# Converting float64 weights 1024 columns at a time, with the sign restored by two leaky ScalarE passes

## The chip, the cores and the metric

The kernel runs on one core of a Trainium2 chip. The metric is the device time of one execution in microseconds; the time before is the median of three runs. The profile is of one further execution on the same kind of chip, taken by the hardware profiler. TensorE (PE) multiplies matrices, VectorE (DVE) and ScalarE (ACT) work elementwise, GpSimd (POOL) does some sums, and SyncE (SP) issues every transfer in one queue.

## The reference

```python
scores = (q_c @ k_c.T) / sqrt(64)          # blocks of 64 tokens, 4 x 8 heads, 576 tokens
attn = exp(scores - max(scores)); attn /= sum(attn) + 1e-9
x = (attn @ v_c)                           # as (2304 tokens) x 512
h = x @ moe_w_in                           # 512 -> 2048
x = (s * relu(h)**2 + b) @ moe_w_out       # 2048 -> 512
h = x @ moe2_w_in
out = (relu(h) + log1p(exp(-abs(h)))) @ moe2_w_out
```

The four weight matrices arrive as float64, because scaling by a float64 square root made them so. The kernel reads each float64 as two 32-bit words and makes a float32 of it.

## The kernel before

The work is written as a list of operations. Each has a key (the time at which it is wanted), a cost on each engine that may run it, the operations that it follows and the places in memory that it takes. A planner (`Work.order`) goes through that list with these costs and writes the order of every engine's instructions: at each step it takes the operation that can start first, and among those that can start at the same time the one with the lowest key. The order is fixed when the program is built; on the chip each engine runs its own list in order and waits on semaphores.

The stages, by the core's time: attention over 18 tiles of 128 tokens with the first products of the first layer mixed in (to about 110 us); the first layer's product with `w_in` by seven-product sums of blocks (`quad`, to about 268 us); its product with `w_out` in six blocks (`block`, to 470 us); the second layer's `w_in` (to about 620 us) and its `w_out` (`second_by_blocks`). Each float32 operand is split into a high and a low part (`split`: a ScalarE copy, L505, and a VectorE difference, L514) and multiplied three times.

`convert` makes float32 out of 512 columns of float64 on 128 partitions: a load of 512 KB into a word buffer `f` (two of them, 1024 words each), then, with `hi` and `lo` the two words,

- o1 (L400, VectorE): `(hi >> 20) & 0x7FF`, the exponent, into the scratch buffer `am` (one, 1024 words: half for the exponent, half for the mantissa);
- o2 (L417, ScalarE): Relu that moves the exponent to float32's place and bias;
- o3 (L430, VectorE): `hi & 0xFFFFF | 0x100000`, the mantissa;
- o4 (L444, VectorE): mantissa plus `lo` times 2^-32;
- o5 (L458, VectorE): the sign of `hi` put into the exponent word;
- o6 (L472, VectorE): mantissa times exponent, into the destination.

`weights1` calls it twice for each of the eight slices of an input matrix, into the buffer `wf` (one), then makes four sums on GpSimd (L492) and splits the results. `weights2` calls it twice for each of eight slices of an output matrix. For the first layer (`ph` 0) the result goes to one of three buffers and is stored to `spill`; for the second (`ph` 1) there is one destination at `AT_S2`, four GpSimd sums are made beside it and three stores take it to `forms2`. The same memory is later used by the second layer's `quad` for `s2`, which therefore waits for all these stores (`free_from["s2"]`).

So there are 64 conversions: 16 each for the two matrices of both layers. `turn` keeps those of one stream in order; a load's key lies 12 us ahead of its conversion (`LEAD_F`). The activation table for the exponential is loaded at the start, the one for the second layer's softplus once, at its first use.

Of the kernel before, what the change touches and what calls it, by code (L numbers as in the profile page):

```python
# [8 lines left out]
F32 = mybir.dt.float32  # L9
F32R = mybir.dt.float32r  # L10
U32 = mybir.dt.uint32
# [7 lines left out]
P = 128  # L19
B, H, S, D = 4, 8, 576, 64  # L20
NT = B * S
DM = H * D
# [193 lines left out]
def block_attention_two_layers(  # L216
# [113 lines left out]
    PLACES = {"A": 2, "S": 3, "at": 3, "wf": 1, "f": 2, "am": 1, "s2": 2, "dd": 2, "go": NGO}  # L330
# [6 lines left out]
    base = {"wf": (AT_WF, 2048), "f": (AT_F, 1024), "am": (AT_AM, 1024), "s2": (AT_S2, N)}  # L337
# [41 lines left out]
    def convert(ph, c, part, key, dst, uses=(), w=(), gone=()):  # L379

        chain = "f", part
        f, am = Place("f"), Place("am")
        src = lambda: (w1, w2)[ph][c, part].bitcast(U32)
        ld = load(
            key - LEAD_F,
            lambda: at(f).bitcast(U32),
            src,
            2 * P * DM * 4,
            deps=gone,
            uses=[*uses, f],  # L390
            after=turn.get(chain, ()),
        )
        turn[chain] = [ld]
        words = lambda: at(f).bitcast(U32).rearrange("p (a b) -> p a b", b=2)
        a = lambda: at(am)[:, :DM].bitcast(U32)
        m = lambda: at(am)[:, DM:].bitcast(U32)
        o1 = add(
            {"DVE": dve(DM, True)},
            key,
            lambda e: nc.vector.tensor_scalar(  # L400
                out=a(),
                in0=words()[:, :, 1],
                scalar1=20,
                scalar2=0x7FF,
                op0=ALU.logical_shift_right,
                op1=ALU.bitwise_and,
            ),
            [ld],
            [f, am],
# [3 lines left out]

        o2 = add(
            {"ACT": act(DM)},
            key,
            lambda e: nc.scalar.activation(  # L417
                out=a().bitcast(I32),
                in_=a().bitcast(I32),
                func=AF.Relu,  # L420
                scale=float(1 << 23),
                bias=-float(896 << 23),
            ),
            [o1],
            [am],
        )
        o3 = add(
            {"DVE": dve(DM, True)},
# [10 lines left out]
            [f, am],  # L439
        )  # L440
        o4 = add(
            {"DVE": dve(DM)},
            key,
            lambda e: nc.vector.scalar_tensor_tensor(  # L444
                out=m().bitcast(F32),
# [7 lines left out]
            [f, am],  # L453
        )
        o5 = add(
            {"DVE": dve(DM)},
            key,
            lambda e: nc.vector.scalar_tensor_tensor(  # L458
                out=a(),
                in0=words()[:, :, 1],  # L460
                scalar=0x80000000,
                in1=a(),
# [1010 lines left out]
```

## Time and profile before

| | |
|---|---|
| Time, median of 3 runs | 830.0 us (829.66 to 830.26) |
| Profiled execution, first to last instruction | 834.3 us |
| PE busy | 795.1 us (95%) |
| DVE busy | 654.0 us (78%) |
| ACT busy | 506.4 us (61%) |
| POOL busy | 148.6 us (18%) |
| Moved by DMA | 180.26 MB, 216 GB/s |

The profile gives no time of its execution other than the span from the first to the last instruction, which is 0.5% above the median of the timed runs. Busy shares are means over stages with different limits, so they don't tell what bounds a stage. Transfers and the reading of the queue are not part of busy time.

### The profile page before, as it was taken

To read this page: it belongs to the slowest core of one execution; us is meant where nothing else is said; L and a number is where in the kernel's file an instruction comes from. 1 tells how busy PE (TensorE), PEld (TensorE's weight loads), DVE (VectorE), ACT (ScalarE), POOL (GpSimd) and SP (SyncE) were. 2 spreads that over 40 slices of the span, in tenths; PEclk is the share of its full clock that TensorE was granted. 3 is DMA by queue.
4 is the path that set the end of the run, shared out by engine and by line. 5 is a ranking of instruction groups with operands and counts; after the bars stand their busy time and mean duration, and the time that the engine had idled before them with its cause. 6 is when DMAs were issued, how large, how long until landed. Compare 5 with 4: busy or idle time off the path is not lost.

```text
span 834.3 us, 14524 instructions
## 1 busy us (share of the span) xinstructions
PE 795.1 (95%) x5117; PEld 775.0 (93%) x5117; DVE 654.0 (78%) x1174; ACT 506.4 (61%) x1076; POOL 148.6 (18%) x162
## 2 busy tenths in 40 slices
PE   4688889999999999999999989999999999999998
PEld 3577789999998999999999989999999999999997
DVE  5799888888967869888888776778784767777865
ACT  3655555666656877767767655555555655555543
POOL 4254240111111003222213540111110000000000
PEclk9899999999999999999999999999999999999999
DMA  8665347868757835767662027657667996688851
GB/s 235 195 190 170 106 144 241 262 240 269 257 218 275 324 107 161 244 225 255 224 197 88 11 95 262 232 197 251 246 233 253 354 372 226 203 262 297 277 187 57
DMA packets 80632, 180.26 MB, mean 216 GB/s; under 512 B 9008, under 2 KB 53040, under 8 KB 79664
## 3 DMA queue, kind: packets, MB, share of 16 engines
q1 hardware_dynamic: 80560, 179.34, 63.9%
q8 instruction: 40, 0.66, 0.3%
q14 instruction: 32, 0.26, 0.1%
HBM read 111.15 MB, written 68.16 MB: 215 GB/s over the span
## 4 chain that ended last, share of the span: by engine, by line
PE 83%; DVE 8%; DMA 3%; ACT 3%; issue 1%; POOL 1%; SPq 0%; ACTq 0%; DVEq 0%
PE at L916 17%; PE S L916 10%; PE S L1093 9%; PE at L1093 9%; PE S L1244 8%; PE at L1244 8%; PE A L916 7%; PE A L1093 6%; PE A L1244 5%; DVE operands L514 2%; DVE mem L492 2%; PE at L852 2%; PE at L733 1%; DMA mem<-in_w_dram 1%; DMA last<-in_k_dram 1%
## 5 line engine op out<-in xcount | busy, mean ns | idle before, releaser
L492 POOL TENSOR_TENSOR mem<-mem 128x256 f32<-128x256 f32 x120 | 109.6, 923 | 414.1 <-DVE mem L472 309.2
L514 DVE TENSOR_TENSOR operands<-mem,operands 128x384 fp32r<-128x384 f32 (+4 forms) x186 | 130.9, 720 | 45.0 <-ACT operands L505 43.1
L505 ACT CAST operands<-mem 128x384 fp32r<-128x384 f32 (+4 forms) x186 | 112.3, 620 | 58.8 <-PE at L1244 36.1
L514 DVE TENSOR_TENSOR operands<-last,operands 128x384 fp32r<-128x384 f32 (+2 forms) x184 | 110.5, 616 | 42.4 <-ACT operands L505 39.9
L505 ACT CAST operands<-last 128x384 fp32r<-128x384 f32 (+2 forms) x184 | 94.3, 528 | 73.2 <-PE A L1093 46.5
L916 PE MATMUL at<-operands 128*128 128x384 f32 x624 | 122.4, 340 | 4.1 <-ACT mem L350 2.0
L916 PEld LDWEIGHTS at<-operands 128*128 128x128 f32 x624 | 110.4, 190 | 6.7 <-ACT mem L350 2.7
L1093 PE MATMUL S<-operands 128*128 128x384 f32 x432 | 90.7, 335 | 0.4 <-DVE operands L514 0.4
L1093 PE MATMUL at<-operands 128*128 128x384 f32 x432 | 90.3, 334 | 0.0
L1244 PE MATMUL S<-operands 128*128 128x384 f32 x384 | 87.4, 334 | 0.1
L1244 PE MATMUL at<-operands 128*128 128x384 f32 x384 | 87.1, 334 | 0.0
L916 PE MATMUL S<-operands 128*128 128x384 f32 x420 | 83.5, 337 | 0.9 <-DVE S L492 0.8
L1093 PEld LDWEIGHTS S<-operands 128*128 128x128 f32 x432 | 76.2, 188 | 0.9 <-DVE operands L514 0.6
L1093 PEld LDWEIGHTS at<-operands 128*128 128x128 f32 x432 | 76.2, 188 | 0.0
L948 ACT ACTIVATE mem<-S 128x384 f32<-128x384 f32 x104 | 50.6, 492 | 41.1 <-PE S L916 34.4
L916 PEld LDWEIGHTS S<-operands 128*128 128x128 f32 x420 | 73.5, 188 | 1.5 <-DVE S L492 1.3
L1244 PEld LDWEIGHTS S<-operands 128*128 128x128 f32 x384 | 68.3, 188 | 0.4 <-DVE operands L514 0.4
L1244 PEld LDWEIGHTS at<-operands 128*128 128x128 f32 x384 | 68.3, 188 | 0.0
L916 PE MATMUL at<-last,operands 128*128 128x384 f32 x336 | 67.2, 337 | 0.6 <-ACT S L938 0.2
L492 DVE TENSOR_TENSOR mem<-mem 128x384 f32<-128x384 f32 (+1 forms) x108 | 60.7, 589 | 9.1 <-ACT mem L948 7.8
L1093 PE MATMUL A<-operands 128*128 128x384 f32 x288 | 65.4, 334 | 0.0
L916 PE MATMUL A<-operands 128*128 128x384 f32 x300 | 60.5, 341 | 3.3 <-ACT S L938 1.5
(79 smaller groups left out, 1217.0 us busy)
## 6 DMA issues: line engine op xcount, KB each, us to landing
mem<-in_w_dram SPq DMA_DIRECT2D x64, 512.0 KB, 4.4
summed<-mem SPq DMA_DIRECT2D x168, 192.0 KB, 2.3
mem<-summed SPq DMA_DIRECT2D x30, 768.0 KB, 4.8
hid<-mem SPq DMA_DIRECT2D x96, 192.0 KB, 2.9
last<-hid SPq DMA_DIRECT2D x24, 768.0 KB, 5.3
last<-summed SPq DMA_DIRECT2D x12, 768.0 KB, 4.9
mem<-forms SPq DMA_DIRECT2D x7, 1024.0 KB, 7.1
last<-in_q_dram SPq DMA_DIRECT2D x18, 256.0 KB, 4.2
```

What stands on the lines that cost most here:

```text
L492: lambda e: on(e).tensor_tensor(out=out(), in0=x(), in1=y(), op=op or ALU.subtract),
L505: lambda e: nc.scalar.copy(out=hi().bitcast(F32R), in_=x()),
L514: lambda e: nc.vector.tensor_tensor(out=lo().bitcast(F32R), in0=x(), in1=hi(), op=ALU.subtract),
L733: nc.tensor.matmul(out_[c * D : (c + 1) * D, pr], of("q")[:, pr * P + c * D : pr * P + (c + 1) * D], kb[:, :, pr, c, :], start=True, stop= ...
L852: nc.tensor.matmul(at(px)[y, x], of("v")[y, x], of("aT")[y, x], start=True, stop=True)
L916: nc.tensor.matmul(acc(dst)().rearrange("p (u c) -> p u c", u=GROUP), l[a], r[c], start=start and kk == 0 and x == 0, stop=kk == 1 and x == 2,
L948: lambda e: nc.scalar.activation(out=at(go), in_=acc(place)(), func=AF.Softplus if ph else AF.Relu),
L1093: nc.tensor.matmul(at(accs[d])[:, :N], l[a], r[c], start=m == 0 and z == 0, stop=m == NM - 1 and z == 2,)
L1244: nc.tensor.matmul(at(accs[d])[:, :N], l[a], r[c], start=i == 0 and y == 0, stop=i == NF - 1 and y == 2,)
```

## The change

Two chunks of 512 columns are converted together. The word buffer `f` becomes one of 2048 words that takes two loads; the scratch `am` holds the exponents of all 1024 columns, and the mantissa is made in the destination instead. For three of the four matrices the shift is arithmetic and keeps the sign (so exponent and sign are one number), and two ScalarE passes with a leaky function (slope 1 on one side, 2^-40 on the other, which rounding drops) turn that number into the float32 word with its sign; the first of them writes over the words, so it follows o4. For the second layer's input matrix the steps stay as they were, 1024 columns wide. The first layer's `weights2` gets a word buffer of its own at `AT_XO` and two destinations in place of three; the second layer's keeps its one destination, which is now written from o3 on.

```diff
-    PLACES = {"A": 2, "S": 3, "at": 3, "wf": 1, "f": 2, "am": 1, "s2": 2, "dd": 2, "go": NGO}
+    PLACES = {"A": 2, "S": 3, "at": 3, "wf": 1, "f": 1, "am": 1, "s2": 2, "dd": 2, "go": NGO}
...
-    base = {"wf": (AT_WF, 2048), "f": (AT_F, 1024), "am": (AT_AM, 1024), "s2": (AT_S2, N)}
+    base = {"wf": (AT_WF, 2048), "f": (AT_F, 2048), "am": (AT_AM, 1024), "s2": (AT_S2, N)}
...
-    def convert(ph, c, part, key, dst, uses=(), w=(), gone=()):
+    def convert(ph, i, part, key, dst, uses=(), w=(), gone=(), words_at=None):
...
+        am, uses = Place("am"), list(uses)
+        if words_at is None:
+            place = Place("f")
+            f, held, fw = lambda: at(place), [place], []
+        else:
+            f, held, fw = lambda: mem(words_at, 2048), [], [(words_at, 2048)]
+        ld = []
+        for y in range(2):
+            c = 2 * i + (y if part else 1 - y)
+            ld.append(
+                load(
+                    key - LEAD_F,
+                    lambda y=y: f()[:, y * 1024 : (y + 1) * 1024].bitcast(U32),
+                    lambda c=c: (w1, w2)[ph][c, part].bitcast(U32),
+                    2 * P * DM * 4,
+                    deps=gone,
+                    uses=[*uses, *held],
+                    after=ld or turn.get(chain, ()),
+                    w=[(z + y * 1024, 1024) for z, _ in fw],
+                )
+            )
+        turn[chain] = ld[1:]
+        words = lambda: f().bitcast(U32).rearrange("p (a b) -> p a b", b=2)
+        a, m, n = lambda: at(am).bitcast(U32), lambda: dst().bitcast(U32), 2 * DM
+        signed = not (ph and part == 0)
...
-                scalar2=0x7FF,
-                op0=ALU.logical_shift_right,
+                scalar2=-1 if signed else 0x7FF,
+                op0=ALU.arith_shift_right,
...
             [o1],
-            [f, am],
+            [*held, *uses],
+            r=fw,
+            w=w,
...
+        if signed:
+
+            y = lambda: f()[:, :n]
+            o2 = add(
+                {"ACT": act(n)},
+                key,
+                lambda e: nc.scalar.activation(
+                    out=y(), in_=a().bitcast(I32), func=AF.Prelu, scale=-1.0, bias=-896.0, alpha=2.0**-40
+                ),
+                [o1, o4],
+                [am, *held],
+                w=fw,
+            )
+            o5 = add(
+                {"ACT": act(n)},
+                key,
+                lambda e: nc.scalar.activation(
+                    out=a().bitcast(I32),
+                    in_=y(),
+                    func=AF.Prelu,
+                    scale=-(2.0**63),
+                    bias=-float(1792 << 23),
+                    alpha=2.0**-40,
+                ),
+                [o2],
+                [am, *held],
+                r=fw,
+            )
...
-        c1 = convert(ph, 2 * i + 1, 0, key, lambda: at(wf)[:, :DM], [wf])
-        c0 = convert(ph, 2 * i, 0, key + 0.1, lambda: at(wf)[:, DM : 2 * DM], [wf])
+        c0 = c1 = convert(ph, i, 0, key, lambda: at(wf)[:, : 2 * DM], [wf])
...
-        x = ((AT_XO, 3) if ph == 0 else (AT_S2, 1))
-        a = x[0] + i % x[1] * 2 * DM
+        a = AT_S2 if ph else AT_XO + 2048 + i % 2 * 2 * DM
...
+        c = [convert(ph, i, 1, key, lambda: mem(a, 2 * DM), (), span, gone, None if ph else AT_XO)]
```

## Rows read from the trace of the kernel before

**Rows 1.** The page: busy time by engine, and the chain that ended last.

```profile
PE 795.1 (95%) x5117; PEld 775.0 (93%) x5117; DVE 654.0 (78%) x1174; ACT 506.4 (61%) x1076; POOL 148.6 (18%) x162
...
PE 83%; DVE 8%; DMA 3%; ACT 3%; issue 1%; POOL 1%; SPq 0%; ACTq 0%; DVEq 0%
```

**Rows 2.** Busy time by stretches: from:to, length, PE, PEld, DVE, ACT, POOL busy, clock, DMA, GB/s.

```profile
0.00:40.00 40.00, 22.32 (x229) 17.93 (x229) 25.54 (x50) 19.94 (x96) 13.97 (x23) 0.94 0.78 221
40.00:98.00 58.00, 50.13 (x754) 43.24 (x752) 54.74 (x107) 33.36 (x68) 25.53 (x27) 0.95 0.49 152
112.00:140.00 28.00, 26.43 (x147) 24.82 (x146) 24.05 (x42) 16.47 (x34) 4.72 (x5) 1.00 0.63 211
140.00:240.00 100.00, 99.34 (x569) 98.69 (x568) 88.68 (x149) 62.34 (x124) 14.78 (x17) 1.00 0.77 256
290.00:470.00 180.00, 180.00 (x1041) 180.00 (x1040) 150.18 (x270) 123.68 (x251) 46.01 (x46) 1.00 0.55 177
```

**Rows 3.** Groups by line, the conversion: count | busy us, mean ns | idle before.

```profile
L458 DVE SCALAR_TENSOR_TENSOR mem<-mem 128x512 uint32<-128x512 uint32 x64 | 46.0, 719 | 1.8 <-ACT mem L417 1.7
L444 DVE SCALAR_TENSOR_TENSOR mem<-mem 128x512 f32<-128x512 uint32 x64 | 45.8, 716 | 0.7
L472 DVE SCALAR_TENSOR_TENSOR mem<-mem 128x512 f32<-128x512 f32 x64 | 44.1, 688 | 1.0
...
L417 ACT ACTIVATE mem<-mem 128x512 int32<-128x512 int32 x64 | 40.3, 630 | 10.1 <-DVE mem L400 9.8
...
L400 DVE TENSOR_SCALAR mem<-mem 128x512 uint32<-128x512 uint32 x64 | 35.3, 552 | 5.5 <-DMA mem<-in_w_dram 4.5
L430 DVE TENSOR_SCALAR mem<-mem 128x512 uint32<-128x512 uint32 x64 | 33.3, 521 | 0.0
```

**Rows 4.** Groups by line and shape: instructions of 1024 columns.

```profile
L514 DVE TENSOR_TENSOR operands<-mem,operands 128x1024 fp32r<-128x1024 f32 x22 | 27.6, 1256 | 4.2 <-ACT operands L505 4.2
...
L505 ACT CAST operands<-mem 128x1024 fp32r<-128x1024 f32 x22 | 23.1, 1050 | 0.4 <-POOL mem L492 0.4
```

**Rows 5.** Line 400, the shift: least, median and greatest duration in ns.

```profile
L400 DVE TENSOR_SCALAR mem<-mem x64: 411/426/1032, 7.9 to 609.5; 128x512 uint32<-128x512 uint32 x64
```

**Rows 6.** Groups by line, VectorE, from 33 to 98 us.

```profile
L458 DVE SCALAR_TENSOR_TENSOR mem<-mem 128x512 uint32<-128x512 uint32 x2 | 2.2, 1121 | 0.0
...
L444 DVE SCALAR_TENSOR_TENSOR mem<-mem 128x512 f32<-128x512 uint32 x2 | 2.0, 988 | 0.0
L472 DVE SCALAR_TENSOR_TENSOR mem<-mem 128x512 f32<-128x512 f32 x2 | 1.5, 739 | 0.0
L400 DVE TENSOR_SCALAR mem<-mem 128x512 uint32<-128x512 uint32 x2 | 1.4, 725 | 0.5 <-DMA mem<-in_w_dram 0.5
...
L430 DVE TENSOR_SCALAR mem<-mem 128x512 uint32<-128x512 uint32 x2 | 0.8, 396 | 0.0
```

**Rows 7.** Line 430, from 140 to 240 us.

```profile
L430 DVE TENSOR_SCALAR mem<-mem x22: 414/422/967, 142.8 to 237.3; 128x512 uint32<-128x512 uint32 x22
```

**Rows 8.** Timeline, 331 to 471 us: start, duration, engine, line, operation.

```profile
331.89 2.89 SPq L367 DMA_DIRECT2D forms<-mem  x3
...
399.11 0.69 DVE L472 SCALAR_TENSOR_TENSOR mem<-mem 128x512 f32<-128x512 f32 x1
...
404.03 2.43 POOL L492 TENSOR_TENSOR mem<-mem 128x256 f32<-128x256 f32 x3 [3.18 <-DVE mem L472]
...
407.27 1.92 SPq L367 DMA_DIRECT2D forms<-mem  x3
...
414.51 0.68 DVE L472 SCALAR_TENSOR_TENSOR mem<-mem 128x512 f32<-128x512 f32 x1
...
439.91 1.47 SPq L367 DMA_DIRECT2D forms<-mem  x3
...
470.69 3.28 PE L916 MATMUL at<-operands 128*128 128x384 f32 x18
```

**Rows 9.** Timeline, ScalarE at 475 us: a table load.

```profile
475.08 1.28 ACT L948 ACT_TABLE_LOAD   x1 [0.20 <-issue]
```

More of the change, by code (lines that the diff above doesn't have):

```diff
@@ L377, in block_attention_two_layers @@
     turn = {}
-    def convert(ph, c, part, key, dst, uses=(), w=(), gone=()):
+    def convert(ph, i, part, key, dst, uses=(), w=(), gone=(), words_at=None):
         chain = "f", part
[L382 to L396, printed above, removed]
+        am, uses = Place("am"), list(uses)
[23 more added lines that the diff above has]
+        signed = not (ph and part == 0)
@@ L412, in convert @@
         turn["am", part] = [o1]
[L414 to L426, printed above, removed]
         o3 = add(
-            {"DVE": dve(DM, True)},
+            {"DVE": dve(n, True)},
             key,
@@ L452, in convert @@
             [o3],
-            [f, am],
-        )
[L455 to L462, printed above, removed]
-                op0=ALU.bitwise_and,
-                op1=ALU.bitwise_or,
-            ),
-            [o2],
-            [f, am],
-        )
+            [*held, *uses],
+            r=fw,
+            w=w,
+        )
@@ new lines, in convert @@
+        if signed:
[14 more added lines that the diff above has]
+                lambda e: nc.scalar.activation(
+                    out=a().bitcast(I32),
+                    in_=y(),
[5 more added lines that the diff above has]
+                [o2],
+                [am, *held],
+                r=fw,
+            )
+        else:
+            o2 = add(
+                {"ACT": act(n)},
+                key,
+                lambda e: nc.scalar.activation(
+                    out=a().bitcast(I32),
+                    in_=a().bitcast(I32),
+                    func=AF.Relu,
+                    scale=float(1 << 23),
+                    bias=-float(896 << 23),
+                ),
+                [o1],
+                [am],
+            )
+            o5 = add(
+                {"DVE": dve(n)},
+                key,
+                lambda e: nc.vector.scalar_tensor_tensor(
+                    out=a(),
+                    in0=words()[:, :, 1],
+                    scalar=0x80000000,
+                    in1=a(),
+                    op0=ALU.bitwise_and,
+                    op1=ALU.bitwise_or,
+                ),
+                [o2],
+                [am, *held],
+                r=fw,
+            )
@@ L469, in convert @@
         return add(
-            {"DVE": dve(DM)},
+            {"DVE": dve(n)},
             key,
@@ L473, in convert @@
                 out=dst(),
-                in0=m().bitcast(F32),
+                in0=dst(),
                 scalar=2.0**-20,
@@ L542, in weights2 @@
     def weights2(ph, i, key):
-        x = ((AT_XO, 3) if ph == 0 else (AT_S2, 1))
-        a = x[0] + i % x[1] * 2 * DM
+        a = AT_S2 if ph else AT_XO + 2048 + i % 2 * 2 * DM
         span = [(a, DM), (a + DM, DM)]
         gone = [o for j in range(NG) for o in x_ready[0, j]] if ph == 0 else quads_done[0]
-        c = [
-            convert(
-                ph, 2 * i + y, 1, key + 0.1 * y, lambda y=y: mem(*span[y]), (), span[y : y + 1], gone
-            )
-            for y in range(2)
-        ]
+        c = [convert(ph, i, 1, key, lambda: mem(a, 2 * DM), (), span, gone, None if ph else AT_XO)]
         if ph == 0:
```

12 lines of the change are left out of this document (5 added, 7 removed).

## The prediction

> **What bounds the kernel now.** I read the page first, then the busy time by stretches, then the groups of the conversion's own lines, then the order of instructions around two places where those lines meet a buffer. TensorE is busy for 795.1 of 834.3 us and carries 83% of the chain that ended last; VectorE carries 8% of that chain [rows 1]. A cheaper VectorE instruction is therefore worth something only where TensorE is idle, and the stretches say where that is [rows 2]. In 0 to 40 us TensorE is idle for 17.7 us, but VectorE works only 25.5 of those 40: that stretch waits for the first transfers. In 40 to 98 us TensorE is idle for 7.9 us while VectorE is busy for 54.7 of 58 us: this stretch, the attention with the first feed-forward products mixed in, is VectorE's. In 112 to 140 us 1.6 us are idle. In 140 to 240 us it is 0.7 us and in 290 to 470 us nothing at all, although VectorE and ScalarE have much to do there. So of some 39 us of idle TensorE only about 10 (7.9 and 1.6) stand where a lighter VectorE can reach them.
>
> **The work taken away.** A conversion of 512 columns has five VectorE instructions and one on ScalarE, 64 times. By the means that is 552 + 521 + 716 + 719 + 688 ns = 3.20 us of VectorE, or 6.39 us for what is now one pair of chunks, and 204.5 us in all; ScalarE spends 40.3 us [rows 3]. For 1024 columns the trace has a two-input VectorE instruction at 1256 ns and a ScalarE pass at 1050 ns [rows 4]. The shift at 1024 columns is not shown: it costs more than the 0.43 us of 512 columns and at most twice that, 0.85 us [rows 5]. I take 0.7, since a two-input instruction doubled in width went from 0.69 to 1.26 and so kept a fixed part.
>
> A signed pair then has two shift-like instructions at 0.7 and two two-input ones at 1.26: 3.9 us (3.4 to 4.2) in place of 6.39. The eight unsigned pairs of the second layer's first matrix keep the sign on VectorE: 5.2 us. Total: 24 x 3.9 + 8 x 5.2 = 135 us in place of 204.5, so VectorE loses some 69 us. ScalarE makes 48 + 8 passes of 1.05 us, 59 us in place of 40: 19 us more. Most of both changes nothing, because 180.0 of 180 us in one of the stretches are already TensorE's [rows 2]; this is what hides them. If that cover were gone, ScalarE would still have 56 us free in those 180.
>
> The shift's mean of 552 ns against a median of 426 and a maximum of 1032 [rows 3, 5] says that some of these instructions run into something that holds them for half a microsecond. The Trainium skill, SBUF — State Buffer, section "Who interferes with whom", says that a VectorE instruction in a two-port mode and a GpSimd one exclude each other for the whole instruction. By that rule the delay comes once per collision and 32 wide shifts collide less often than 64 narrow ones, half of 64 x 0.126 = 8 us, 4 us of VectorE less in the whole kernel; if the delay grew with the width instead, those 4 us would stay. No row of this trace has both widths of the shift.
>
> **What it is worth in the attention stretch.** Only one pair of chunks (the second slice of first-layer weights) is converted between 33 and 98 us, stretched over the whole of it since its priority is low. Its ten VectorE instructions took 2.2 + 2.0 + 1.5 + 1.4 + 0.8 = 7.9 us [rows 6]. After the change it is one pass of 3.9 us: 4.0 us less in a stretch whose bound is VectorE (2.5 us less, if I take the mean price of a pair instead). It also ends the conversion earlier: the second half no longer queues for the single scratch buffer behind the first. Against that, the shift now waits for both transfers. The first half's wait is already 0.5 us [rows 6], and a second 512 KB at the 221 GB/s of the start [rows 2] lands 2.4 us later; if the planned order does not foresee this, VectorE, which runs in order, stands for up to 2.4 us with the attention's reductions and subtractions queued behind it and the next scores' turn waiting for those. I charge 1.0. The first pair, at the very start, waits in the same way, but there TensorE waits for transfers anyway, and its products start much later; I charge nothing, and at most the same 2.4 us. Net for this stretch: -3.0 us (from -4.0 to +1).
>
> **112 to 140 us.** Two signed streams are converted here; VectorE goes from 24.1 of 28 us to about 20, ScalarE from 16.5 to about 19 [rows 2]. Of 1.6 us of idle TensorE I count 0.5 as won (between 0 and 1.6). Wider instructions make others wait longer behind them, but 1256 and 1050 ns already occur 22 times each [rows 4], so this is no new length.
>
> **What is added: longer holds.** Three resources are held longer, and each could become a wait. The scratch buffer is held from the shift to the last product: 0.7 + 0.7 + 1.26 + 1.05 + 1.05 + 1.26 = 6.0 us without waits. In 142.8 to 237.3 us 22 conversions started, one in 4.5 us [rows 7], of which 0.43 + 0.42 + 3 x 0.7 = 2.95 are instructions and 1.55 waits. For a pair that is 9.0 us before; after it is 6.0 plus between 1.5 and 4 of waits, 7.5 to 10, and I take 9.0: no change. The single word buffer means that a pair's load starts only when the pair before has left it; the loads' lead covers that outside the stretch below. SyncE's queue, on which hidden blocks and stores stand behind such a load, then moves by as much.
>
> In 290 to 470 us the second layer's output weights go round one destination buffer: convert, four sums on GpSimd, store three pieces, and only then may the next pair write there. Before, only the last instruction writes it, so the next pair is converted up to there while the stores run. After the change the mask writes it, three steps earlier. The cycle before: 4.92 us from the last product of a first half (399.11) to the three sums behind the second half (404.03; the fourth sum was done early), 2.43 us for these, 8.05 us until the next write at 414.51; 15.4 us [rows 8]. The first piece holds 0.69 + 0.43 + 0.42 + 3 x 0.69 = 3.6 us of instructions, so 1.3 of waits. After: 0.7 + 1.26 + 2.1 + 1.26 = 5.3 us and 1.3 to 2.5 of waits, all four sums 4 x 0.81 = 3.25, the same 8.05: 18.5 us (17.9 to 19.1). Eight rounds, with the first stores at 331.9, then have the last at 331.9 + 7 x 18.5 = 461.4 in place of 439.9, landed at 468.7 (7.2 us later, as from 407.27 to 414.51). The next product begins at 470.7 and needs that memory soon after [rows 8]. So I cost this at nothing, with 2 us to spare.
>
> **Sum.** -3.0 - 0.5 = -3.5 us on the profiled execution's 834.3, so 830.8. The median of the timed runs is 830.0, 0.5% below that execution; scaled by 830.8 / 834.3 the forecast is 826.5 us.
>
> **Rivals.**
> *Nothing comes through.* The pair in the attention stretch loses to the wait for its second half what it gains, or TensorE's idle time there belongs to a latency (scores, maximum, exponential, turn) and not to VectorE's load. For it: 7.9 us of idle TensorE beside 3.3 us of idle VectorE [rows 2]. Against it: VectorE at 94%. Time: 830.0, chance 0.20.
> *More than forecast.* With the second weight slice ready some 30 us earlier its products fill TensorE's gaps between the tiles, and most of the 7.9 + 1.6 us go. Against it: those products need VectorE too. Time: 822, chance 0.08.
> *The store round decides (slower).* If the cycle in 290 to 470 us passes 18.8 us, the last stores land after 470.7 and every further microsecond of cycle costs seven. At 20 us: 331.9 + 140 + 7.2 = 479.1, 8.4 us late, less the 3.5 won: 835. For it: my own upper end is 19.1. Against it: a lighter VectorE shortens the waits, and the first pair, converted in one pass, may start sooner. Chance 0.16.
> *The scratch buffer decides (slower).* At 10 us for a pair, eleven pairs in 140 to 240 us end 11 us late, in a stretch where TensorE has 0.7 us of slack [rows 2]; if half of that shows, 830 + 5.5 - 3.5 = 832, up to 837. Chance 0.07.
> *Table switching.* No leaky pass is in this trace. If the leaky function and the exponential had to be reloaded for each other, each load would cost 1.28 us of ScalarE [rows 9]; two pairs are converted among the exponentials, at most eight loads, 10 us, in a stretch where ScalarE is busy 33.4 of 58 us [rows 2]. A third of it showing takes the gain back: 830. The Trainium skill, ScalarE activation tables: per-element evaluation and per-set limits, section "What a function is on this engine", has the rule: functions of different sets are one table load apart, those of one set need no switch, and it gives the 1283 ns that the row shows. It names no set for this function. Chance 0.03.
>
> **Numbers.** Forecast 826.5 (own range 823.5 to 828.3) with 0.46. A measurement of this kernel can tell about 0.2%, 1.7 us. Faster: 0.46 + 0.08 = 0.54; same: 0.20 + 0.03 = 0.23; slower: 0.16 + 0.07 = 0.23. The range from 821.5 to 834.0 leaves out the best part of the large gain and the upper half of the two slow cases, less than 0.2.
>
> **What the profile after would show.** 32 shifts near 0.7 us, 56 ScalarE passes near 1.05 us, VectorE's busy time down by 60 to 70 us and ScalarE's up by 19. TensorE's idle time in 40 to 98 us down by some 3 us, and every later mark (the end of the first product, the start of the second layer) earlier by as much. The stores of the second layer's weights 18 to 19 us apart, the last landing before the second layer's first product. I am wrong if that product waits at about 470 us, if TensorE shows idle time in 140 to 240 us, or if a shift stands for microseconds on a transfer during the attention. More than two table loads would mean switching.

## Result and the profile after

The changed kernel takes 838.62 us (median of four runs, 836.19 to 839.47) against 830.13 us for the kernel before beside it: a ratio of 1.0088, with a 95% interval from 1.0064 to 1.0112 (the two medians by themselves give 1.0102, inside it). It is slower by 8.5 us, where 826.5 was forecast, and it lies above the range.

The profiled execution of the changed kernel lasted 837.7 us, only 3.4 us more than that of the kernel before. The latter was a long one for its kernel: 834.3 us against a median of 830.0, although the spans of the changed kernel's four runs lie 1.8 us below their times. So a comparison of these two shows less than half of the loss; further down two profiles that show all of it are compared.

The page after, busy time and chain, answers [rows 1]:

```profile
PE 800.2 (96%) x5117; PEld 777.5 (93%) x5117; DVE 607.5 (73%) x990; ACT 525.3 (63%) x1068; POOL 154.8 (18%) x162
...
PE 78%; DVE 11%; ACT 3%; issue 3%; DMA 2%; POOL 2%; SPq 1%; ACTq 0%; DVEq 0%; POOLq 0%
```

VectorE's busy time has fallen by 46.5 us, yet its share of the chain that ended last rose from 8 to 11%. On this one chain it works less and is waited for more. The groups by line answer [rows 3]; the shift is now L410, the mask L427, the low word L443, the last product L516, the leaky passes L462 and L472, and the unsigned pairs' two steps L488 and L501:

```profile
L443 DVE SCALAR_TENSOR_TENSOR mem<-mem 128x1024 f32<-128x1024 uint32 x32 | 42.4, 1324 | 0.4
L516 DVE SCALAR_TENSOR_TENSOR mem<-mem 128x1024 f32<-128x1024 f32 x32 | 39.1, 1223 | 11.0 <-ACT mem L472 10.7
L427 DVE TENSOR_SCALAR mem<-mem 128x1024 uint32<-128x1024 uint32 x32 | 25.5, 796 | 0.0
L462 ACT ACTIVATE mem<-mem 128x1024 f32<-128x1024 int32 x24 | 25.4, 1060 | 6.3 <-DVE mem L443 6.2
L472 ACT ACTIVATE mem<-mem 128x1024 int32<-128x1024 f32 x24 | 25.3, 1056 | 0.1
L410 DVE TENSOR_SCALAR mem<-mem 128x1024 int32<-128x1024 int32 x32 | 22.7, 710 | 7.1 <-DMA mem<-in_w_dram 6.9
L501 DVE SCALAR_TENSOR_TENSOR mem<-mem 128x1024 uint32<-128x1024 uint32 x8 | 9.7, 1218 | 0.6 <-ACT mem L488 0.6
L488 ACT ACTIVATE mem<-mem 128x1024 int32<-128x1024 int32 x8 | 8.5, 1061 | 0.6 <-DVE mem L410 0.5
```

The conversions' VectorE work is 42.4 + 39.1 + 25.5 + 22.7 + 9.7 = 139.4 us (135 forecast), ScalarE's 59.2 us (59 forecast). The last column has what is new: the last product stood 10.7 us behind the second leaky pass, where the sign step stood 1.7 us behind ScalarE before. The first leaky pass stood 6.2 us behind the low word, and the shift 6.9 us behind its transfers, where it was 4.5 us before [rows 3].

The stretches answer [rows 2]. The three lines behind them are other stretches of this kernel; all have the columns of [rows 2].

```profile
0.00:40.00 40.00, 24.87 (x299) 20.20 (x299) 24.22 (x49) 23.33 (x108) 15.66 (x25) 0.96 0.74 219
40.00:98.00 58.00, 51.90 (x670) 45.91 (x671) 51.88 (x97) 33.77 (x59) 22.74 (x24) 0.88 0.58 174
112.00:140.00 28.00, 25.23 (x126) 23.85 (x127) 13.94 (x19) 15.33 (x30) 2.66 (x3) 0.88 0.43 142
140.00:240.00 100.00, 98.29 (x558) 96.72 (x557) 64.80 (x78) 65.84 (x118) 24.09 (x20) 1.00 0.67 229
290.00:470.00 180.00, 177.56 (x1022) 176.66 (x1021) 141.08 (x220) 133.24 (x253) 44.32 (x46) 1.00 0.57 187
...
40.00:60.00 20.00, 14.02 (x148) 12.29 (x149) 17.44 (x29) 10.84 (x17) 9.09 (x9) 0.66 0.53 156
110.00:120.00 10.00, 6.31 (x23) 5.16 (x22) 8.04 (x11) 4.83 (x10) 4.24 (x5) 0.73 0.31 103
272.00:320.00 48.00, 44.63 (x251) 43.36 (x251) 43.39 (x70) 41.45 (x81) 7.70 (x7) 1.00 0.73 273
```

In 40 to 98 us TensorE's busy time rose from 50.1 to 51.9 us, while the number of its instructions fell from 754 to 670. Neither tells how much work was done: busy time is longer where the granted clock is lower, 0.88 in place of 0.95, and the instructions differ in size. Of the 670, 98 are the first layer's products of 384 columns (L953); of the 754, only 72 were. The rest are the attention's smaller ones. A count can be compared from 105 us on, where the attention's 936 instructions have been begun in both kernels (all but one in the changed one). The first line is the changed kernel, the second the kernel before:

```profile
0.00:105.00 105.00, 83.77 (x1060) 72.50 (x1061) 80.05 (x152) 62.17 (x174) 42.31 (x54) 0.92 0.62 185
0.00:105.00 105.00, 79.20 (x1044) 67.44 (x1045) 85.35 (x166) 58.68 (x174) 40.27 (x51) 0.95 0.60 180
```

So the changed kernel is 16 products ahead when the attention is over. It loses behind that. In 112 to 140 us VectorE is busy for 13.9 us where it was 24.1, and TensorE does less beside it, 126 products in place of 147. Much of the time that VectorE has there is one wait of 7.94 us for a ScalarE copy (start, duration, and in the bracket the idle time before):

```profile
126.78 0.56 DVE L536 TENSOR_TENSOR mem<-A,mem 128x384 f32<-128x384 f32 x1 [7.94 <-ACT S L975]
```

In 290 to 470 us 2.4 us of TensorE are idle where none were.

**Where the clock falls.** VectorE and then TensorE in 37 to 55 us (start, duration, engine, line; the last bracket is the idle time before and what ended it):

```profile
37.12 0.69 DVE L410 TENSOR_SCALAR mem<-mem 128x1024 int32<-128x1024 int32 x1
37.72 1.22 DVE L427 TENSOR_SCALAR mem<-mem 128x1024 uint32<-128x1024 uint32 x1
38.86 0.68 DVE L352 COPY mem<-at 128x512 f32<-128x512 f32 x1
39.46 1.21 DVE L443 SCALAR_TENSOR_TENSOR mem<-mem 128x1024 f32<-128x1024 uint32 x1
...
41.46 1.83 DVE L558 TENSOR_TENSOR operands<-mem,operands 128x1024 fp32r<-128x1024 f32 x1
43.21 0.68 DVE L558 TENSOR_TENSOR operands<-at,operands 128x512 fp32r<-128x512 f32 x1
```

```profile
39.96 1.09 PE L770 MATMUL at<-last 128*64 128x128 f32 x16 [0.21 <-ACT last L794]
44.04 1.09 PE L870 MATMUL at<-ident,last 128*128 128x128 f32 x4 [2.99 <-DVE operands L558]
45.05 1.97 PE L770 MATMUL at<-last 128*64 128x128 f32 x16
46.96 1.97 PE L889 MATMUL at<-last 64*64 64x64 f32 x32
51.25 3.68 PE L770 MATMUL at<-last 128*64 128x128 f32 x32 [2.32 <-DVE last L816]
```

The second slice's conversion is not spread over the attention any more. Its wide steps follow one another between 37.1 and 40.7 us, ahead of the 0.68 us split at 43.21 for which TensorE waits 2.99 us. The step right before that split, 1.83 us at 41.46 us, is one of 1024 columns, of which the kernel before has as many [rows 4]. The score products behind it (L770) then take 1.97 us for sixteen where they took 1.09 at 39.96 us, and the granted clock of 40 to 60 us is 0.66: TensorE, having stood, runs part of this stretch at the lower of its two levels. At 60 us it has begun 445 instructions where the kernel before has begun 495, but by 105 us it is ahead by the 16 above. So this loss is made good before the attention ends.

**Where the weights come late.** Line 410 from 140 to 240 us answers [rows 7] (least, median and greatest ns, then first and last start):

```profile
L410 DVE TENSOR_SCALAR mem<-mem x10: 685/694/695, 142.4 to 235.6; 128x1024 int32<-128x1024 int32 x10
```

Nine intervals in 93.2 us are 10.4 us for a pair; before it was 9.0 (two chunks of 4.5). VectorE on one of the second layer's unsigned pairs, and TensorE beside it:

```profile
292.83 0.69 DVE L410 TENSOR_SCALAR mem<-mem 128x1024 int32<-128x1024 int32 x1
...
297.29 1.22 DVE L516 SCALAR_TENSOR_TENSOR mem<-mem 128x1024 f32<-128x1024 f32 x1
298.43 1.28 DVE L558 TENSOR_TENSOR operands<-last,operands 128x512 fp32r<-128x512 f32 x2
299.64 1.70 DVE L359 TENSOR_SCALAR last<-last,s_sb,b_sb 128x384 f32<-128x384 f32 x2
301.26 1.48 DVE L558 TENSOR_TENSOR operands<-mem,operands 128x768 fp32r<-128x768 f32 x1
302.66 1.54 DVE L558 TENSOR_TENSOR operands<-last,operands 128x384 fp32r<-128x384 f32 x2
```

```profile
301.18 0.44 PE L1130 MATMUL S<-operands 128*128 128x384 f32 x1
303.79 1.14 PE L1130 MATMUL S<-operands 128*128 128x384 f32 x5 [2.17 <-DVE operands L558]
```

From 292.8 to 304.2 us VectorE is without a gap; TensorE waits 2.17 us for a split that stands behind the conversion, its activations and a 768-column split.

**The store round.** The stores of the second layer's output weights, issued (x24 in the first line of this answer), answer [rows 8]:

```profile
L367 SPq DMA_DIRECT2D forms<-mem x24: 370/427/562, 317.7 to 441.3; - x24
```

### The profile page after: what moved, and what is told of

It reads as the page before. It is cut to its first block, busy times and chain, and to the rows that moved or that the text cites. A ratio compares the mean times of both kernels' runs of the same rounds, so it can differ in the third digit from the quotient of the medians.

```text
span 837.7 us, 14342 instructions
## 1 busy us (share of the span) xinstructions
PE 800.2 (96%) x5117; PEld 777.5 (93%) x5117; DVE 607.5 (73%) x990; ACT 525.3 (63%) x1068; POOL 154.8 (18%) x162
## 4 chain that ended last, share of the span: by engine, by line
PE 78%; DVE 11%; ACT 3%; issue 3%; DMA 2%; POOL 2%; SPq 1%; ACTq 0%; DVEq 0%; POOLq 0%
PE at L953 14%; PE S L953 9%; PE at L1130 8%; PE A L953 8%; PE S L1281 8%; PE S L1130 8%; PE at L1281 8%; PE A L1130 5%; PE A L1281 5%; DVE mem L536 3%; PE at L889 2%; PE at L770 2%; DVE operands L558 2%; DVE last L558 2%; POOL mem L536 1%
## 5 line engine op out<-in xcount | busy, mean ns | idle before, releaser
L536 POOL TENSOR_TENSOR mem<-mem 128x256 f32<-128x256 f32 x120 | 117.3, 997 | 400.3 <-DVE mem L516 371.3
L558 DVE TENSOR_TENSOR operands<-last,operands 128x384 fp32r<-128x384 f32 (+2 forms) x184 | 113.4, 629 | 49.6 <-ACT operands L549 44.8
L953 PE MATMUL at<-operands 128*128 128x384 f32 x624 | 122.6, 338 | 1.6 <-ACT S L975 0.9
L953 PEld LDWEIGHTS at<-operands 128*128 128x128 f32 x624 | 109.2, 188 | 4.9 <-ACT S L975 2.2
L953 PE MATMUL S<-operands 128*128 128x384 f32 x420 | 84.2, 340 | 2.9 <-ACT S L975 1.8
L953 PEld LDWEIGHTS S<-operands 128*128 128x128 f32 x420 | 74.3, 190 | 3.8 <-ACT S L975 2.1
L536 DVE TENSOR_TENSOR mem<-mem 128x384 f32<-128x384 f32 (+1 forms) x108 | 59.9, 577 | 15.4 <-ACT mem L985 13.0
L953 PE MATMUL at<-last,operands 128*128 128x384 f32 x336 | 67.2, 337 | 2.1 <-ACT S L975 1.5
L1130 PE MATMUL A<-operands 128*128 128x384 f32 x288 | 65.2, 334 | 0.0
L953 PE MATMUL A<-operands 128*128 128x384 f32 x300 | 63.0, 351 | 1.9 <-DVE A L536 0.8
```

Of the source, the lines that this page charges most:

```text
L536: lambda e: on(e).tensor_tensor(out=out(), in0=x(), in1=y(), op=op or ALU.subtract),
L558: lambda e: nc.vector.tensor_tensor(out=lo().bitcast(F32R), in0=x(), in1=hi(), op=ALU.subtract),
L953: nc.tensor.matmul(acc(dst)().rearrange("p (u c) -> p u c", u=GROUP), l[a], r[c], start=start and kk == 0 and x == 0, stop=kk == 1 and x == 2,
L1130: nc.tensor.matmul(at(accs[d])[:, :N], l[a], r[c], start=m == 0 and z == 0, stop=m == NM - 1 and z == 2,)
```

## Experiments

All ratios are to the kernel before, on the same chip. e1 to e4 ran together, then e5 to e8, e9 to e12, e13 to e16, and e17 with e18.

**One half of the change each, the second slice later, and the planner's constant.**

e1 is the changed kernel with the sign on VectorE in all matrices (wide, no leaky pass; the change's buffers stay):
```diff
-        signed = not (ph and part == 0)
+        signed = False
```


> The changed kernel with the sign put in by VectorE everywhere (24 more wide VectorE instructions, 24 fewer ScalarE passes). Theory W (the wide steps and the long holds make the loss at places where VectorE is tight): 838 to 843, since VectorE gets 29 us more. Theory S (the two leaky ScalarE passes make the loss): 832 or less. Theory O (the planner's order, which differs everywhere after any edit, makes it): anything from 828 to 842.

e2 is the kernel before, 512 columns at a time, with the two leaky passes (and their wait for o4) in place of Relu and the sign step:
```diff
+            y = lambda: at(f)[:, :DM]
...
+                    out=y(), in_=a().bitcast(I32), func=AF.Prelu, scale=-1.0, bias=-896.0, alpha=2.0**-40
+                ),
+                [o1, o4],
+                [f, am],
```


> The kernel before, 512 columns at a time with its two word buffers, with only the sign moved to two leaky ScalarE passes. Theory W: 830 or below, since VectorE has 17 us less work and no step is wider. Theory S: 834 or more. Theory O: anything from 826 to 838.

e3 makes the load of the second slice follow the attention's tile 11:
```diff
-        c0 = c1 = convert(ph, i, 0, key, lambda: at(wf)[:, : 2 * DM], [wf])
+        late = [tile_done[11]] if ph == 0 and i == 1 else ()
+        c0 = c1 = convert(ph, i, 0, key, lambda: at(wf)[:, : 2 * DM], [wf], (), late)
...
+        tile_done[t] = o10
```


> The changed kernel with the loads of the second weight slice held until tile 11 of the attention is through, so that no wide step stands at 37 to 44 us. Theory W: 833 to 836, with the first dip of the clock shorter. Theory S: 838, no change. Theory O: anything from 832 to 842.

e4 changes only the time that the planner assumes for a handoff between engines, in the kernel before, and so the order that it writes:
```diff
-    SAME, OTHER, LOAD = 0.13, 0.15762, 2.0
+    SAME, OTHER, LOAD = 0.13, 0.16, 2.0
```


> The kernel before with one planner constant changed (0.15762 to 0.16 us for a wait between engines): the same instructions, another order. Theories W and S: 828.5 to 831.5, as this touches neither the steps nor the engines. Theory O: off by 3 us or more in either direction.

Measured: e1 1.0094 (1.0057 to 1.0130), e2 1.0093 (1.0064 to 1.0122), e3 1.0190 (1.0153 to 1.0226), e4 0.9987 (0.9962 to 1.0011). Each half alone costs as much as both together. So neither is the whole cause, and the cost isn't a sum of parts. That the conversion of the second slice stands in the attention's way is seen above, but moving it back cost another 1%. By 105 us TensorE had then begun 1037 instructions, against 1060 in the changed kernel and 1044 before. I take it that the slice then comes too late; no run shows this by itself. e3's time lies above everything that was expected for it.

**The leaky passes beside the mantissa; each half of the shift behind its own transfer.**

In e5 both leaky passes work in place in the scratch buffer, so they needn't follow o4 and run beside the mantissa's steps; e6 does so in e2's kernel:
```diff
-            y = lambda: f()[:, :n]
+            y = lambda: at(am)
...
-                [o1, o4],
-                [am, *held],
+                [o1],
+                [am],
```
In e7 the shift is two instructions of 512 columns, each behind its own transfer (`[ld[y]]` in place of `ld`); e8 is e5 and e7 together.

> The changed kernel with both leaky passes in place in the scratch buffer, so that they run beside the mask and the low word's step on VectorE instead of behind them. Theory H (the four steps in a row, VectorE to ScalarE to ScalarE to VectorE, make each engine's fixed order stand for the other): 831 to 835, and the waits of the last product on the second leaky pass in 110 to 262 us, 7 us, mostly gone. Theory D (the shift now waits for two transfers, which the planner takes for faster than they are): 837 to 841, no change. Theory O (order alone): anything.

> The 512-column kernel with leaky passes, these again beside VectorE's steps. Theory H: back to 828 to 834 from 842.7, as nothing then stands in a row and VectorE has 17 us less than before. Theories D and W do not touch this kernel. Theory O: anything from 828 to 843.

> The changed kernel with the shift issued as two instructions of 512 columns, each behind its own transfer. Theory D: 834 to 836, the 7 us for which the shift stands on transfers fall to 4 or less. Theory H: 838 to 840, since the chain of four is as long. Theory O: anything.

> The changed kernel with both edits: leaky passes beside VectorE's steps and the shift in halves. Theories H and D together: 826 to 832, as fast as the kernel before or faster. If only one of them holds: that one's time, 831 to 836. Theory O: anything.

Measured: e5 1.0079 (1.0056 to 1.0102), e6 1.0057 (1.0034 to 1.0080), e7 1.0123 (1.0087 to 1.0160), e8 1.0090 (1.0056 to 1.0125). For e5, e6 and e8 the theory of the four steps in a row expected up to 835, 834 and 832 us, and for e7 the theory of the transfers up to 836; all were slower. e7 and e8 don't take the wait for the transfers away: their shifts stand 11.8 and 19.3 us on them, where the changed kernel's stand 6.9 and 4 or less were expected. So they neither show nor exclude a cost of the second transfer. With 512 columns the step from e2 to e6 is 1.0093 to 1.0057, but the intervals overlap, so a share of the four steps in a row isn't shown there; in the wide kernel their removal isn't told from no change. Each edit also gives another order, and orders alone differ by up to 1.6% (below), so one run of each can't exclude a cause of this size. What the four steps do to the cycle, line 410 of e5 does show, from 140 to 240 us:

```profile
L410 DVE TENSOR_SCALAR mem<-mem x11: 682/694/1241, 141.7 to 230.8; 128x1024 int32<-128x1024 int32 x11
```

Ten intervals in 89.1 us: 8.9 us for a pair, as before the change, in place of 10.4. The longer cycle comes from the leaky passes' wait for o4, inside the hold of the scratch buffer. (e5 frees the word buffer earlier as well, so the two holds aren't told apart.) The kernels of 512 columns agree: 11.3 us for two chunks in e2, 9.0 in e18, which is e6 in another order.

**Other orders.** e9 is the changed kernel with 0.16 as in e4; e10 and e11 are the changed kernel and the kernel before with 0.14 and 0.17; e12 is e6 with 0.16; e13 and e14 (after, before) have 0.12 and 0.15, e15 and e16 (after, before) 0.14 and 0.18; e17 is e1 and e18 is e6, both with 0.12 and 0.15. The edit is e4's line with other numbers.

> The changed kernel with one planner constant changed (0.15762 to 0.16 us between engines): the same instructions in another order, as was done to the kernel before. Theory O (the loss is that of one unlucky order): anything from 828 to 842, and below 834 in one of this run and the next. Theory L (the conversions' longer path costs in every order): 836 to 842 in both.

> The changed kernel with two planner constants changed (0.13 to 0.14 and 0.15762 to 0.17 us), a third order of the same instructions. Theory O: anything from 828 to 842. Theory L: 836 to 842.

> The kernel before with the same two constants changed. Theory O: off by 4 us or more from 830, since its own order would be the lucky one. Theory L: 828 to 834, as with the first change of a constant.

> The 512-column kernel with leaky passes beside VectorE's steps (838.0 us), with the constant at 0.16: another order, and a profile of it. Theory O: below 834 or above 841. Theory S (ScalarE's added passes cost): 836 to 840 again, with TensorE waiting on ScalarE's copies before 285 us.

> The changed kernel; only the planner's two assumed handoff times differ (0.12 and 0.15 us in place of 0.13 and 0.15762), so each engine runs the same instructions in another order. Theory O (the change's own work is free, the changed kernel's time depends strongly on which order is written): somewhere between ratio 0.997 and 1.018, and not within 0.002 of the changed kernel's 1.0088. Theory C (the change costs some 0.8% in an ordinary order and the one order at parity was luck): 1.006 to 1.012.

> The kernel before with the same two planner constants (0.12, 0.15). Theory O in its strong form (only the changed kernel's time hangs on the order): ratio 0.997 to 1.003, as in the two other orders measured. Rival (every kernel of this planner scatters by a per cent, and the orders of before tried so far happened to lie close together): outside of 0.995 to 1.005.

> The changed kernel with assumed handoff times of 0.14 and 0.18 us. Theory O: between 0.997 and 1.018, and over the five orders of the changed kernel a spread of at least 0.012. Theory C: 1.006 to 1.012.

> The kernel before with assumed handoff times of 0.14 and 0.18 us. Theory O in its strong form: 0.997 to 1.003, so that the five orders of this kernel spread by less than 0.005. Rival (any order of this planner may cost a per cent): outside of 0.995 to 1.005.

> Pairs of 1024 columns without the leaky passes (the sign stays on VectorE in all four matrices), with assumed handoff times of 0.12 and 0.15 us. At these constants the kernel before measured 0.9959 and the changed kernel 1.0085. If the width and the longer holds are what costs (theory W), this lies at 1.004 to 1.012, near the changed kernel; if the leaky passes with their two handoffs cost (theory S), near before, 0.995 to 1.000; if the two share it, 1.000 to 1.004.

> 512 columns at a time with the leaky passes kept beside the mantissa's steps, at the same constants (0.12 and 0.15). Theory W: near the kernel before, 0.995 to 1.000. Theory S: near the changed kernel, 1.004 to 1.012. Shared: 1.000 to 1.004.

Measured ratios, one column for each order (the assumed handoff to another engine):

| kernel | 0.15 | 0.1576 | 0.16 | 0.17 | 0.18 |
|---|---|---|---|---|---|
| before | 0.9959 (e14) | 1 | 0.9987 (e4) | 0.9983 (e11) | 1.0000 (e16) |
| 512 columns, leaky passes beside | 0.9979 (e18) | 1.0057 (e6) | 1.0019 (e12) | | |
| 1024 columns, sign on VectorE | 1.0068 (e17) | 1.0094 (e1) | | | |
| the change | 1.0085 (e13) | 1.0088 | 1.0154 (e9) | 0.9992 (e10) | 1.0094 (e15) |

Half a 95% interval is 0.0020 to 0.0051, widest in e9, which runs from 1.0103 to 1.0204. Column by column the change costs 1.26, 0.88, 1.67, 0.09 and 0.94%, 0.97% on average. So it isn't free in an ordinary order, and the one at parity (e10 against e11) is the best of five; the theory that the change's own work is free and only the order matters falls. It had also excluded e13's 1.0085. e9 lies above everything that was expected for it, and e14 between the two theories that were set for it. But the same instructions lie 1.6% apart, and those of the kernel before 0.4%. The width together with its buffers (one word buffer, the mantissa in the destination, two destinations for the first layer's output weights) costs 1.1 and 0.9%, nearly all of 1.26 and 0.88; no run parts the width from the buffers. The leaky passes beside VectorE's steps, with 512 columns, cost 0.2, 0.6 and 0.3%. The fastest kernel of the study is the one before in another order: e14, 828.26 us, 0.9959 (0.9939 to 0.9979).

e13 and e14 share their constants and differ by 10.6 us in their profiles as well (835.9 and 825.3 us). Their stretches, e13 first:

```profile
105.00:140.00 35.00, 31.84 (x168) 29.81 (x168) 20.65 (x29) 20.26 (x41) 5.72 (x6) 0.95 0.48 167
140.00:240.00 100.00, 98.30 (x560) 97.05 (x559) 65.10 (x75) 67.40 (x120) 25.29 (x20) 1.00 0.65 221
240.00:330.00 90.00, 86.01 (x479) 84.10 (x478) 71.83 (x110) 69.49 (x136) 13.07 (x14) 0.98 0.78 273
```

```profile
105.00:140.00 35.00, 34.18 (x193) 32.83 (x192) 30.12 (x55) 21.20 (x43) 6.39 (x6) 1.00 0.65 213
140.00:240.00 100.00, 99.02 (x567) 98.19 (x566) 87.94 (x147) 62.43 (x122) 18.68 (x20) 1.00 0.75 242
240.00:330.00 90.00, 89.42 (x513) 88.52 (x512) 71.86 (x129) 70.75 (x144) 11.82 (x14) 1.00 0.72 246
```

A product takes 0.173 us where TensorE doesn't wait (1041 in 180.0 us [rows 2]). In 105 to 140 us the changed kernel does 25 fewer, 4.3 us; in 140 to 240 us 7, 1.2 us; in 240 to 330 us 34, 5.9 us. That is 11.4 us. Before 105 us it has done 14 more (1075 against 1061, the attention complete in both), 2.4 us, though its attention's last product starts later (102.5 against 96.2 us). So 52 products, 9.0 us, are missing by 330 us. The second product's last instruction starts 9.0 us later (472.9 against 463.9 us) and the execution ends 10.6 us later, so nearly all is lost in these stretches. The rows also say by what. TensorE's busy time is shorter by 2.3, 0.7 and 3.4 us, 6.5 us in all. The granted clock is 0.95 for 1.00 in 35 us and 0.98 for 1.00 in 90 us, by estimate 1.8 us each. So most of the loss is waiting, and some three tenths of it is the clock.

The same for the others: TensorE instructions begun from the start to four times, and those in 240 to 330 us:

```
kernel                              to 105  to 140  to 240  to 330  240-330  ratio
e14 before                            1061    1252    1817    2328      513  0.9959
e16 before                            1057    1236    1805    2302      499  1.0000
e10 change                            1056    1242    1803    2300      499  0.9992
e18 512, leaky beside                 1067    1229    1789    2299      512  0.9979
e4  before                            1055    1233    1795    2296      503  0.9987
before                                1044    1219    1786    2290      505  1
e11 before                            1049    1221    1790    2287      499  0.9983
e13 change                            1075    1241    1799    2276      479  1.0085
e5  change, leaky beside              1068    1236    1770    2276      508  1.0079
e17 1024, sign on VectorE             1053    1205    1766    2274      510  1.0068
e15 change                            1067    1246    1795    2266      473  1.0094
e8  change, leaky beside, halves      1035    1202    1754    2262      510  1.0090
e2  512, leaky behind o4              1052    1241    1774    2260      488  1.0093
the change                            1060    1217    1773    2257      486  1.0088
e12 512, leaky beside                 1020    1185    1747    2257      512  1.0019
e1  1024, sign on VectorE             1028    1195    1736    2241      507  1.0094
e7  change, halves                    1020    1208    1776    2224      450  1.0123
e3  change, second slice late         1037    1198    1742    2208      468  1.0190
e9  change                            1047    1191    1726    2198      474  1.0154
```

(e6 has no row: its profiled execution lasted 1997 us. At 105 us e7 and e8 still have 36 and 32 small instructions of the attention ahead of them; by 140 us no kernel has any.) The count by 330 us goes with the ratio: 2287 and more up to 1.0000, 2276 and fewer from 1.0068 on. The one exception is e12, whose profiled execution is the longest of its ten (838.64 us, median 836.47). Against the kernel before in the same order, the changed kernel at 105 us is ahead by 16, 14, 10 and 7 products and once behind by 8, on average 1.3 us ahead. By 330 us it is 33, 52, 36 and 98 behind and once 13 ahead, on average 7.1 us behind, of some 8 us that the ratios give. So the change loses after the attention, in the first layer's first product and the start of its second.

The column of 240 to 330 us splits by one feature. Wherever the leaky passes follow o4 it is 450 to 499, everywhere else 499 to 513. By 240 us 26 to 28 chunks are converted in the former (the first layer has 32), 30 to 32 in the latter. The first layer's last pair comes to its first leaky pass at 259 to 286 us in the former, and at 232 to 239 us where the passes run beside (e5, e8, e12, e18). So the weights come late for the second product, which starts at 272.9 us in the changed kernel, and VectorE's work piles up there (43.4 of 48 us busy in 272 to 320 us of the changed kernel). But lateness isn't enough for a loss. e10, at parity, has it too:

```profile
L410 DVE TENSOR_SCALAR mem<-mem x9: 693/694/700, 145.1 to 233.3; 128x1024 int32<-128x1024 int32 x9
```

Eight intervals in 88.2 us are 11.0 us for a pair, 28 chunks are converted by 240 us, the last pair is at its first leaky pass at 259.3 us, and e10 does as many products in 240 to 330 us as e11. The stretches before 240 us don't split by the feature. Kernels without the late weights lose there instead: e5 gave its 22 products in 240 to 330 us back as 22 in 140 to 240 us (536 against 558), and of the 54 that e17 is behind e14 by 330 us, 47 are missing by 140 us.

## Why the prediction was wrong

What failed, in the prediction's own terms, are two steps: the 0.5 us won in 112 to 140 us, and the longer hold of the scratch buffer, which was put at nothing ("I take 9.0: no change"). The gain of 3 us in the attention was there at 105 us. From 105 to 330 us the changed kernel then fell back by 49 products, 8.5 us, in its own order and also on average over the five.

**Work taken away: right by durations, too large in busy time.** 139.4 us of VectorE for 135, 59.2 us of ScalarE for 59, and 0.71 us for the shift at 1024 columns where 0.7 was taken. But VectorE's busy time fell by 46.5 us, where 60 to 70 were to be seen. Durations of neighbours overlap: the shift at 37.12 us ends at 37.81, the mask starts at 37.72. Over all of VectorE's instructions the durations add up to 714.4 us before and 655.4 us after, so they fell by 59.0 us: 65.1 us less in the conversions and 6.1 us more elsewhere. The other 12.5 us are overlaps that went with 184 instructions. No term of the sum hung on this.

The shift's delay beyond its median fell from 8 us in all to 32 x (710 - 688) = 0.7 us. The Trainium skill, SBUF — State Buffer, section "Who interferes with whom", has two-port VectorE work and GpSimd exclude each other for the whole instruction. By that fewer and wider instructions meet such a delay less often, and the trace agrees for the shift; for the mask a larger part stayed, 32 x (796 - 687) = 3.5 of 64 x (521 - 420) = 6.5 us. In the kernel before all 28 shifts and masks of more than 550 ns overlap a GpSimd instruction, of the other 100 only 22.

**The attention: right in size, not by its path.** At 105 us the changed kernel is 16 products ahead, 2.8 us, where the step "Net for this stretch: -3.0 us" had 3. But TensorE's idle time in 40 to 98 us fell only from 7.9 to 6.1 us, the granted clock fell from 0.95 to 0.88, and at 60 us the kernel was 50 instructions behind. It had begun 70 more before 40 us (299 against 229), where the prediction counted nothing. The other orders of the kernel before have 262 to 310 there, and in one order of five the lead at 105 us is a lag, so the size is in part luck. The rival of the early second slice had such a lead as its mechanism; its 822 us didn't come, because the lead was lost behind 105 us. The step had priced the pair as a sum of VectorE time spread over the stretch. The planned order put its steps together ahead of the attention's split. The feared wait for the second transfer isn't seen there: the shift at 37.12 us doesn't wait.

**112 to 140 us: the step "Of 1.6 us of idle TensorE I count 0.5 as won" failed.** It became 21 products fewer, 3.6 us. The premise was that two streams are converted here and keep VectorE busy for about 20 us. In the changed kernel's order one pair ends at 101.8 us and the next begins at 127.25 us (its loads are issued at 118.05 us), where the kernel before begins six chunks between 112.4 and 136.8 us. So it isn't the length of the wide steps that TensorE waits for here; VectorE itself stands 7.94 us. In 110 to 120 us TensorE is idle for 3.7 us and its clock is 0.73. Why this order waits here stays open.

**Longer holds: the step "I take 9.0: no change" failed.** The instructions of a pair are 0.69 + 0.69 + 1.23 + 1.06 + 1.06 + 1.22 = 6.0 us, as forecast; the waits between them were 4.4 us and not 3. The cycle of 10.4 us lies beyond the upper bound of 10 that the prediction had worked out, and the rival of the scratch buffer had this mechanism. It had the wrong place: in 140 to 240 us TensorE is idle for 1.7 us only (one of the signs of being wrong that the prediction had named), and the larger part of the lag comes due behind it, in 240 to 330 us, where the prediction counted nothing. Against the changed kernel, e1, e5, e8 and e17 do 21 to 31 products more in that stretch, 3.6 to 5.4 us (e17 against e13, which has its constants). But e5 shows that taking the lag away doesn't shorten the time by as much, and e10 that an order can carry it without a loss.

**The store round: harmless, as forecast.** Eight rounds from 317.7 to about 437.7 us are 17.1 us a round (18.5 forecast, 15.4 before), and the last store was issued at 441.3 us, well before the second layer's product at about 476 us. That rival, to which most of the slower chance had gone, decided nothing. **Table switching:** two table loads, as before.

**The premise behind the sum.** Each term was a change of one duration in an otherwise fixed course, and where TensorE was 99 to 100% busy nothing was to be lost. But the order of all engines is written anew from new costs, and a TensorE without idle time isn't one with slack: its feeding had little to spare. The 0.4% by which five orders of the same kernel differ is already as large as the predicted gain; with the change it is 1.6%.

**What stays open.** That the width with its buffers costs about 1% in an ordinary order is measured in two orders; which of its waits does it is not. No run takes the waits for the transfers away. The sums at 110 to 120 us (clock 0.73) and the split at 303.8 us are seen in the profile, but only the longer cycle of the scratch buffer was taken away by itself, and that didn't give the time back. No run holds one written order and changes only the width, so order and width can't be separated further here.

## What to carry to other kernels

Where one engine is the bound and the others run through a planned fixed order, work taken off the others can be worth nothing, as here; price also how long the longest step may stand ahead of what the bound engine waits for, and how long the scarcest buffer is held. A cycle that gets longer behind a busy engine isn't free just because that engine shows no idle time there: follow the lag to the stretch where the late piece is first needed. And before a gain of under 1% is believed or a loss explained, time the same kernel in a few other orders, and count what the bound engine has done by several times, from a point on where the instructions counted are of one size: here one constant of the planner was worth as much as the forecast.

## What the hardware showed that was not expected

In the stretch where it stands, TensorE can lose more than the length of its waits. In 40 to 60 us of the changed kernel it was idle for 6.0 us, and the granted clock of the stretch was 0.66, so that sixteen score products took 1.97 us for 1.09; in 110 to 120 us, with 3.7 us idle, it was 0.73. The kernel before has in 40 to 60 us:

```profile
40.00:60.00 20.00, 17.04 (x268) 14.36 (x267) 18.23 (x38) 11.86 (x30) 9.44 (x10) 0.86 0.61 182
```

It is idle there for 3.0 us and has 0.86. But e13 is idle for 6.0 us in this stretch as well, and has 0.83, so the idle time of a stretch doesn't by itself tell the clock. Between the changed kernel and the kernel before the stretches differ by 120 instructions (148 and 268); how many of these the clock cost, and how many the other order of the work, the two rows don't tell. By 105 us all of them were made up.
